# Twelve blocks' convolution on GpSimd in fp32, and stores one block late by SyncE

## The chip, the cores and the metric

The kernel runs on one core of a Trainium2 chip. Its time is the device time of one execution in microseconds (us). The kernel before takes 466.52 us, the median of 13 runs (466.1 to 467.46).

## What is computed

A causal convolution with a window of seven tokens, its weights a softmax for each of eight heads of 24 channels, and behind it a feed-forward layer whose hidden value is the greatest of three products:

```python
w = softmax(weight)                       # [8, 7]
out = einsum('hk,bskhg->bshg', w, x_unf)  # x: [8, 4160, 192], zeros ahead of each sequence
x = out.reshape(33280, 192)
h = maximum(maximum(x @ w1, x @ w2), x @ w3)   # 192 -> 768
return h @ w_out                          # 768 -> 192
```

Inputs and output are fp32.

## The kernel before

**Blocks.** The 33280 tokens are cut into 65 blocks of 512: eight from each of the eight sequences, and one more made of the last 64 tokens of every sequence (it stands at place 58). The loop at L545 takes blocks 2 to 64, one a pass; blocks 0 and 1 are done ahead of it. The order of all instructions on each engine is the order of the program text, written by hand.

**The feed-forward layer.** The maximum is computed as relu(y(w1-w3)), against y(w2-w3), and y w3 is added back through m = w3 w_out. `l1` (L390) does one sixth of the first layer of a block: TensorE multiplies the two halves of `wd` with y (L399, PSUM tiles lp and lq, two products beside each other in the two halves of the rows), ScalarE takes the relu of one (L403, to r), VectorE the maximum of r and the other (L404, to h). `st2` (L408) does one sixth of the second layer of the block before (L451, PSUM tile po); ScalarE copies one half (L460), VectorE adds the other (L461) into the output tile o. A pass t is thus `l1(t, 0..5)` interleaved with `st2(t-1, 0..5)`.

**The convolution.** Blocks 0 to 3 are convolved in another way (`conv_dense`) while the weights arrive. From block 4 on, the path of a block is:

- `load_x` (L113): SyncE loads x in eight rows of 70 tokens (64 and the six before them), six blocks ahead, into six buffers.
- `cast_x` (L147): GpSimd casts it to fp16 in two instructions (L158), five blocks ahead; where a row starts a sequence it sets six rows to zero (L155).
- `conv` (L291): TensorE multiplies it with a band matrix, 16 matmuls of 192 columns (L301), for two blocks at once (block 4 alone), three passes ahead of the first of the two. So every second pass has a convolution in it. The result lies in PSUM tiles G.
- `evac` (L342): ScalarE and VectorE cast G to fp16 tiles ys (L347).
- `turn` (L351): SyncE has the DMA engines transpose ys into yd (L358), channels on the partitions, three blocks ahead.
- `double` (L362): two copies by DMA (L366) bring each half of the partitions the tokens that the other half holds, two blocks ahead. `y_all` and `y_tok` then address the four runs of 128 tokens for L399 and L451.

**Stores.** `store(t-1)` at the end of a pass (L594) is issued by GpSimd (L480), behind that pass's casts; only the last two blocks go by SyncE and ScalarE. The output tiles o are three buffers, taken by `begin`.

**Queues.** SyncE issues, in this order within a pass, the load of t+6, the two doublings of t+2 and the transpose of t+3. Each engine waits in order: what stands behind a waiting instruction waits with it. The DMAs that SyncE issues take eight completion semaphores in turn, so a transfer is issued only when the eighth before it is complete.

Of the kernel before, what the change touches and what calls it, by code (L numbers as in the profile page):

```python
# [9 lines left out]
FP32 = mybir.dt.float32  # L10
FP16 = mybir.dt.float16
# [3 lines left out]
P = 128  # L15
KW = 7
PAD = KW - 1
NHEAD = 8
GRP = 24
# [3 lines left out]
HALF = P // 2  # L23
# [4 lines left out]
def kernel(  # L28
# [12 lines left out]
    nc = tc.nc  # L41
    ctx.enter_context(tc.manual_schedule())

    B, SEQ, D = x.shape
# [6 lines left out]
    blocks = []  # L51
    nfull = SEQ // NBLK
# [14 lines left out]
    if segs:  # L67
        blocks.append(segs)
    NB = len(blocks)
    ENDS = NB - 7  # L70
    blocks.insert(ENDS, blocks.pop())
    blkN = [sum(sg[2] for sg in blk) for blk in blocks]

    def conv_chunks(blk):
# [21 lines left out]
    xap = ctx.enter_context(tc.tile_pool(name="xap", bufs=1))  # L96
    xbp = ctx.enter_context(tc.tile_pool(name="xbp", bufs=1))
    xfp = ctx.enter_context(tc.tile_pool(name="xfp", bufs=6))
    x16p = ctx.enter_context(tc.tile_pool(name="x16p", bufs=3))
    ysp = ctx.enter_context(tc.tile_pool(name="ysp", bufs=3))  # L100
    ydp = ctx.enter_context(tc.tile_pool(name="ydp", bufs=6))
# [9 lines left out]
    xin = {}  # L111

    def load_x(t, eng=nc.sync):  # L113
        if not 0 <= t < NB:
            return
        pool, tag = (xfp, "xf") if t > 1 else ((xap, "xa"), (xbp, "xb"))[t]
        xf = pool.tile([P, NR, D], FP32, tag=tag, name=f"xf_{t}")
        if t < NDENSE:
            todo = [(0, c[3], c[1] * SEQ + c[2]) for c in chunks_of[t]]
        else:  # L120
            todo = [(PAD, HALF, b * SEQ) if s == 0 else (0, HALF + PAD, b * SEQ + s - PAD)
                    for b, s in rows_of(t)]
        parts = []
        i, n = 0, len(todo)
        row = [c[2] for c in todo]
        while i < n:
            k = i
            while k + 1 < n and todo[k + 1][:2] == todo[i][:2] and row[k + 1] - row[k] == row[i + 1] - row[i]:
                k += 1
            step = row[i + 1] - row[i] if k > i else 0  # L130
            p0, rlen = todo[i][:2]
            src = bass.AP(tensor=x.tensor, offset=row[i] * D,
                          ap=[[D, rlen], [step * D, k - i + 1], [1, D]])
            eng.dma_start(out=xf[p0:p0 + rlen, i:k + 1, :], in_=src)  # L134
            if parts and parts[-1][0] == rlen:
                parts[-1] = (rlen, parts[-1][1], k + 1)
            else:
                parts.append((rlen, i, k + 1))
            i = k + 1
        xin[t] = [xf, todo[0][0], parts]  # L140

    def place(t):
        return (t, 0, 1) if t == NDENSE else (t - (t - NDENSE - 1) % 2, (t - NDENSE - 1) % 2, 2)

    x16s, slots = {}, {}

    def cast_x(t):  # L147
        if not 0 <= t < NB:
            return
        xf, p0, _ = xin.pop(t)  # L150
        t0, u, nu = place(t)
        if u == 0:
            x16s[t0] = x16p.tile([P, NHEAD, 2, nu, NR // 2, GRP], FP16, tag="x16", name=f"x16_{t0}")
        if p0:
            nc.gpsimd.memset(xf[0:p0, 0, :], 0.0)  # L155
        K = HALF + PAD
        for c in range(2):
            nc.gpsimd.tensor_copy(out=x16s[t0][0:K, :, c, u, :, :].rearrange("p h r c -> p r h c"),  # L158
                                  in_=xf[0:K, c:NR:2, :].rearrange("p r (h c) -> p r h c", c=GRP))

    NC, NSLOT, CYC = D // HALF, D // 32, 96
    NCH = NC * NBLK // P
# [69 lines left out]
    cast_dense(0, (nc.vector.tensor_copy, nc.gpsimd.tensor_copy))  # L234
    for v in range(2):
        nc.gpsimd.memset(xz[1][v][:], 0.0)
    bps = psq.tile([32, WIN, NHEAD], FP32, tag="q", name="band_cols")
    for c in range(WIN):
        nc.tensor.matmul(bps[:, c, :], lhsT=line[:, WIN - 1 - c:WIN + 31 - c],
# [111 lines left out]
    def turn(t):  # L351


        if t >= NB:
            return
        t0, u, nu = place(t)
        yd = dense[t] = ydp.tile([P, 2, NCH // 2, P], FP16, tag="yd", name=f"yd_{t}")
        nc.sync.dma_start_transpose(out=yd[:, 0, :, :],  # L358
                                    in_=slots[t0][:, u, :, :].rearrange("p r d -> p (r d)"))
# [6 lines left out]
                nc.sync.dma_start(out=yd[HALF * i:HALF * (i + 1), 1, :, :],  # L366
                                  in_=yd[HALF * (1 - i):HALF * (2 - i), 0, :, :])

    def spot(i, f):

        return f // 2 + (0 if f % 2 == i else NCH // 2)

    def y_all(t, i, c):
        row = slice(HALF * i, HALF * (i + 1))
        if t < NDENSE:
            return dense[t][row, c, :]
        a = dense[t][row, 0, 0, :]
        s0, s1 = spot(i, c), spot(i, c + NC)
        assert all(spot(i, NC * r + c) == (s1 if r % 2 else s0) + NC * (r // 2) for r in range(4))
        return bass.AP(tensor=a.tensor, offset=a.offset + P * s0,  # L380
                       ap=[list(a.ap[0]), [P * NC, 2], [P * (s1 - s0), 2], [1, P]])

    def y_tok(t, i, c, s):
        row = slice(HALF * i, HALF * (i + 1))
        if t < NDENSE:
            return dense[t][row, c, P * s:P * (s + 1)]
        k = spot(i, NC * s + c)
        return dense[t][row, k // (NCH // 2), k % (NCH // 2), :]

    def l1(t, j, pools=((psp, "p"), (psq, "q"))):  # L390

# [93 lines left out]
    def begin(t):  # L485
        hs[t] = hp.tile([P, NJ, NBLK], FP16, tag="h", name=f"h_{t}")
        outs[t] = outp.tile([P, 4, D], FP32, tag="o", name=f"o_{t}")
# [52 lines left out]

    convs_at = {2: 4, 3: 5}
    doubles_at = {2: (), 3: (4,), 4: (5, 6)}
    for t in range(2, NB):  # L545
        if t > 4:
            load_x(t + 6)
        for u in doubles_at.get(t, (t + 2,)):
            double(u)
        if t == 4:  # L550
            load_x(t + 6)
        if t > 3:
            cast_x(t + 5)
        begin(t)
        l1(t, 0)
        if t == 2:
            conv_dense(3, (nc.scalar.copy, nc.vector.tensor_copy, nc.scalar.copy))
            cross_dma(3)
            load_x(7)
        u = convs_at.get(t, t + 3 if t % 2 == 0 else NB)  # L560
        if t > 2 and u < NB:
            st2(t - 1, 0, NJ, True)
        conv(u, PQ if t == 2 else WPWQ)
        if t == 2:
            evac(u, 0)
            evac(u, 1, nc.vector.tensor_copy)
        else:
            for i in (0, 1):
                evac(u, i)
            for i in (3, 2):  # L570
                evac(u, i, nc.vector.tensor_copy)
        if t == 2:
            turn(4)
            load_x(8)
            cast_x(5)
            cast_x(6)
        elif t == 3:
            turn(5)
            turn(6)
            load_x(9)  # L580
            cast_x(7)
            cast_x(8)
        else:
            turn(t + 3)
        st2(t - 1, 0, NJ)
        for j in range(1, NJ):
            l1(t, j)
            st2(t - 1, j, NJ)
            if t == NB - 1 and j == 3:
                store(t - 1, 0, 2, (nc.sync,))  # L590
        if t == NB - 1:
            store(t - 1, 2, 4, (nc.sync,))
        else:
            store(t - 1, 0, 4, (nc.gpsimd,))  # L594
    for u in range(NJ):
        st2(NB - 1, u, NJ)
# [28 lines left out]
```

## Time and profile before

| what | value |
|---|---|
| median of 13 runs | 466.52 us |
| time of the profiled execution | 467.46 us |
| its span, first to last instruction | 465.7 us |
| TensorE busy, of it the convolution of blocks from 4 on (L301) | 459.3, 26.1 us |
| VectorE, ScalarE, GpSimd busy | 359.7, 318.6, 163.6 us |
| GpSimd: casts of x (L158), store issues (L480) | 97.7 us x122, 48.2 us x64 |
| GpSimd waiting ahead of a store for L461 | 214.4 us |
| SyncE waiting ahead of a transpose for the evacuation (L347) | 114.3 us |
| one transpose issue, one load issue, one doubling issue on SyncE | 1.29, 0.52, 0.50 us (median, 150 to 260 us) |
| DMA: SyncE's queue, GpSimd's queue, share of 16 engines | 57.9%, 15.0% |
| moved | 81.14 MB, 174 GB/s |
| TensorE's granted clock | 1.00 throughout |

A line of the profile names line, engine and operation, then output and inputs by the program's names, with partitions x elements; "x61" is a count, the number after the bar the busy time, then the mean of one in ns, then the engine's idle time ahead of it and what ended that. In the timeline a line is start, duration, engine, line and operation, in us from the span's start. PE is TensorE (PEld its weight loads), DVE VectorE, ACT ScalarE, POOL GpSimd, SPq the issues of SyncE.

### The profile page before, as it was taken

Reading aid. Unit: us, or ns where it says so; the run is one execution under the profiler, and the core shown is the slowest. Engines: PE = TensorE matmul, PEld = TensorE weight load, DVE = VectorE, ACT = ScalarE, POOL = GpSimd, SP = SyncE. Lnnn points to the kernel's source line nnn. Section 1 sums busy time; section 2 is a strip of 40 time slices with the busy share of each in tenths; the row PEclk is TensorE's granted clock in tenths of the full one; section 3 lists DMA queues with packets and bytes.
Section 4 is the critical chain, followed back from the end, with each engine's and each line's share of the span. In section 5 each row is a group of like instructions: output and inputs, shape, how many; then the busy total and the mean of one; then the engine's idle time right before and its main releaser. Section 6 shows DMA issues by size and latency. Waiting matters only on the chain.

```text
span 465.7 us, 17191 instructions
## 1 busy us (share of the span) xinstructions
PE 459.3 (99%) x7065; PEld 372.0 (80%) x7065; DVE 359.7 (77%) x607; ACT 318.6 (68%) x609; POOL 163.6 (35%) x227
## 2 busy tenths in 40 slices
PE   8899999999999999999999999999999999999996
PEld 4487878788788888878788887878888787887886
DVE  7778777877878777777777877778778787787775
ACT  5766767667666676676766767676676766766664
POOL 5664343244234324423424432432442343243010
PEclk9999999999999999999999999999999999999999
DMA  8949987778687777888766868778686976774512
GB/s 199 236 115 196 216 211 188 174 196 176 166 212 183 151 186 176 184 180 198 184 148 194 175 175 197 174 176 188 171 183 165 208 171 167 183 169 107 119 69 103
DMA packets 107114, 81.14 MB, mean 174 GB/s; under 512 B 53110, under 2 KB 101980, under 8 KB 107036
## 3 DMA queue, kind: packets, MB, share of 16 engines
q1 hardware_dynamic: 99804, 55.17, 57.9%
q0 software_dynamic: 7072, 24.78, 15.0%
q8 instruction: 55, 0.90, 0.9%
q14 instruction: 23, 0.19, 0.1%
q10 hardware_dynamic: 160, 0.10, 0.1%
HBM read 30.28 MB, written 25.56 MB: 120 GB/s over the span
## 4 chain that ended last, share of the span: by engine, by line
PE 94%; DMA 3%; SPq 2%; issue 0%; POOL 0%; DVE 0%; ACT 0%
PE lq L399 38%; PE po L451 36%; PE lp L399 15%; PE G L301 6%; DMA wos<-in_moe_w_out_dram 3%; SPq L190 1%; PE D L319 0%; SPq L134 0%; POOL wo L525 0%; PE pm L280 0%; PE pm L284 0%; DVE o L461 0%; ACT a L460 0%
## 5 line engine op out<-in xcount | busy, mean ns | idle before, releaser
L404 DVE TENSOR_TENSOR h<-r,lq 128x512 f16<-128x512 f16 x386 | 264.7, 686 | 98.4 <-ACT r L403 97.9
L403 ACT ACTIVATE r<-lp 128x512 f16<-128x512 f32 x386 | 230.5, 597 | 134.5 <-PE lp L399 122.9
L399 PE MATMUL lp<-yd,wd 64*128 64x512 f16 x1158 | 312.2, 376 | 0.7 <-DVE wd L256 0.5
L399 PE MATMUL lq<-yd,wd 64*128 64x512 f16 x1158 | 312.1, 376 | 0.0
L451 PE MATMUL po<-wo,h 64*128 64x192 f16 x3120 | 262.6, 243 | 0.0
L451 PEld LDWEIGHTS <-h 64*128 64x128 f16 x3120 | 208.4, 94 | 20.5
L399 PEld LDWEIGHTS <-wd 64*128 64x128 f16 x2340 | 161.9, 94 | 37.2 <-issue 1.4
L480 POOL DMA_DIRECT2D out_dram<-o x64 | 48.2, 753 | 280.6 <-DVE o L461 214.4
L451 PE MATMUL po<-m,yd 64*128 64x192 f16 x780 | 109.5, 243 | 0.0
L158 POOL CAST x<-xf 70x768 f16<-70x768 f32 x122 | 97.7, 835 | 2.3 <-PE po L451 1.8
L461 DVE TENSOR_TENSOR o<-a,po 128x384 f32<-128x384 f32 (+1 forms) x132 | 71.3, 541 | 0.6 <-ACT a L460 0.6
L451 PEld LDWEIGHTS <-yd 64*128 64x128 f16 x780 | 61.7, 94 | 12.0
L460 ACT COPY a<-po 128x384 f32<-128x384 f32 (+1 forms) x132 | 62.2, 472 | 2.1 <-PE po L451 2.1
L347 DVE CAST ys<-G 128x384 f16<-128x384 f32 x61 | 31.0, 549 | 0.0
L301 PEld LDWEIGHTS <-band 70*64 70x64 f16 x496 | 19.5, 109 | 11.5 <-PE lp L399 11.4
L347 ACT CAST ys<-G 128x384 f16<-128x384 f32 x61 | 26.2, 482 | 0.0
L301 PE MATMUL G<-x,band 70*64 70x192 f16 (+1 forms) x496 | 26.1, 248 | 0.0
L215 PE MATMUL idle<-idle 128*128 128x512 f16 x15 | 6.5, 578 | 1.2 <-DVE idle L210 1.2
L177 POOL CAST xz<-xf 112x80 f16<-112x80 f32 (+2 forms) x18 | 5.2, 332 | 4.0 <-DMA xf<-in_x_dram 3.2
L319 PEld LDWEIGHTS <-xz 112*32 112x32 f16 x240 | 4.6, 107 | 2.1 <-POOL xz L177 0.8
L319 PE MATMUL D<-band,xz 112*32 112x103 f16 (+1 forms) x240 | 5.3, 229 | 0.0
L335 DVE COPY yd<-yd 64x512 f16<-64x512 f16 x9 | 4.2, 468 | 0.5 <-ACT yd L325 0.2
(45 smaller groups left out, 52.0 us busy)
## 6 DMA issues: line engine op xcount, KB each, us to landing
xf<-in_x_dram SPq DMA_DIRECT2D x57, 420.0 KB
out_dram<-o POOLq DMA_DIRECT2D x62, 384.0 KB, 3.7
yd<-yd SPq DMA_DIRECT2D x122, 96.0 KB
xf<-in_x_dram SPq DMA_DIRECT2D x7, 367.5 KB
ws<-in_moe_w_dram SPq DMA_DIRECT2D x6, 192.0 KB
yd<-ys SPq DMA_TRANSPOSE x61
w3s<-in_moe_w_dram SPq DMA_DIRECT2D x3, 192.0 KB
wos<-in_moe_w_out_dram SPq DMA_DIRECT2D x1, 576.0 KB
```

The costliest lines, as they stand in the source:

```text
L158: nc.gpsimd.tensor_copy(out=x16s[t0][0:K, :, c, u, :, :].rearrange("p h r c -> p r h c"), in_=xf[0:K, c:NR:2, :].rearrange("p r (h c) -> p ...
L215: nc.tensor.matmul(ps[:], lhsT=idle[:, 0:P], rhs=idle[:], start=True, stop=True)
L301: nc.tensor.matmul(G[h // per][HALF * c:HALF * (c + 1), h % per, :], lhsT=band[0:HALF + PAD, h, PAD:HALF + PAD], rhs=x16s[t0][0:HALF + PAD ...
L319: nc.tensor.matmul(ps[32 * g:32 * g + 32, lo:hi], lhsT=xz[t][v][0:rlen, q, 32 * s:32 * s + 32], rhs=band[0:rlen, h, cc:cc + hi - lo], star ...
L347: copy(out=slots[t][:, :, :, GRP * per * i:GRP * per * (i + 1)].rearrange("p u r (h c) -> p h (u r) c", c=GRP), in_=G[i][:].rearrange("p h ...
L399: nc.tensor.matmul(ps[i][:, 0:N], lhsT=wd[row, c, P * j:P * (j + 1)], rhs=y_all(t, i, c), start=(c == 0), stop=(c == NC - 1))
L403: nc.scalar.activation(out=r[:, 0:N], in_=ps[0][:, 0:N], func=AF.Relu)
L404: nc.vector.tensor_max(out=hs[t][:, j, 0:N], in0=r[:, 0:N], in1=ps[1][:, 0:N])
L451: nc.tensor.matmul(ps[b0, i][:, s % 2, :], lhsT=a, rhs=b, start=first, stop=last)
L460: nc.scalar.copy(out=a[:, ss, :], in_=ps[s0, 0][:, ss, :])
L461: nc.vector.tensor_add(out=outs[t][:, s0:s + 1, :], in0=a[:, ss, :], in1=ps[s0, 1][:, ss, :])
L480: qs[0].dma_start(out=bass.AP(tensor=out.tensor, offset=r * D, ap=[[D, n], [step * D, s1 - s0], [1, D]]), in_=ob[p0:p0 + n, s0:s1, :])
```

## The change

Twelve blocks leave the path above: those at places 11, 16, 21, ... 61 and 64. The eight blocks of the last sequence and four of the one before it are put there in their order, so that each block finds the end of the one before it in its sequence. The others keep their path in 24 pairs and block 4 alone; the convolution of a pair still comes three passes ahead of its first.

A block q of the twelve is loaded as four rows of 128 tokens without overlap (`load_q`), into the buffers of blocks 0 and 1. GpSimd casts it (`cast_q`), SyncE transposes it before the convolution (`turn_q`), so that tokens lie along the free axis, and copies the six tokens ahead of each run into a strip in front (`lead_q`; a small copy on GpSimd does the strips of the odd runs). Then GpSimd computes a tap at a time (`tap_q`): three multiplications of 128x256 by a number for each partition, fp16 to fp32, and from the second tap on an addition of 128x768 in fp32; the last addition writes yd in fp16. Doubling, `l1` and `st2` are as for the others.

The load is issued six passes ahead of the first tap, the casts three, the transpose two, the strips one. The taps are spread over five passes as 2, 1, 2, 1, 1 and end three passes before the block is used. The first of the twelve (11) is loaded in pass 2 behind the loads of blocks 7 and 8, cast in pass 3, transposed in pass 4, and its taps lie in passes 5 to 8 as 2, 2, 2, 1. The last (64) has its taps in passes 58 to 61. The weights by channel (`spread_w`) go through DRAM in passes 3 and 4.

The stores of all blocks but block 0 are now issued by SyncE, a pass later: `store(t-2)` behind the transpose of pass t.

```diff
...
     NB = len(blocks)
+    EVERY = 5
+    qpos = [q for q in range(11, NB - 3, EVERY)] + [NB - 1]
+    qset = set(qpos)
     ENDS = NB - 7
-    blocks.insert(ENDS, blocks.pop())
+    ends = blocks.pop()
+    lanes = blocks[-nfull:] + blocks[-2 * nfull:-nfull]
+    lanes, rest = lanes[:len(qpos)], [blk for blk in blocks if blk not in lanes[:len(qpos)]]
+    rest.insert(ENDS - sum(q < ENDS for q in qpos), ends)
+    blocks = [(lanes if t in qset else rest).pop(0) for t in range(NB)]
     blkN = [sum(sg[2] for sg in blk) for blk in blocks]
...
     xfp = ctx.enter_context(tc.tile_pool(name="xfp", bufs=6))
+    xqp = ctx.enter_context(tc.tile_pool(name="xqp", bufs=2))
+    xtp = ctx.enter_context(tc.tile_pool(name="xtp", bufs=3))
+    accp = ctx.enter_context(tc.tile_pool(name="accp", bufs=2))
     x16p = ctx.enter_context(tc.tile_pool(name="x16p", bufs=3))
...
     def load_x(t, eng=nc.sync):
-        if not 0 <= t < NB:
+        if not 0 <= t < NB or t in qset:
             return
...
         xin[t] = [xf, todo[0][0], parts]
+    pairs, left = {}, [t for t in range(NDENSE + 1, NB) if t not in qset]
+    assert len(left) % 2 == 0
+    for a in left[::2]:
+        b = left[left.index(a) + 1]
+        assert b == a + 1
+        pairs[a], pairs[b] = (a, 0, 2), (a, 1, 2)
+    pairs[NDENSE] = (NDENSE, 0, 1)
     def place(t):
-        return (t, 0, 1) if t == NDENSE else (t - (t - NDENSE - 1) % 2, (t - NDENSE - 1) % 2, 2)
+        return pairs[t]
     x16s, slots = {}, {}
     def cast_x(t):
-        if not 0 <= t < NB:
+        if not 0 <= t < NB or t in qset:
             return
...
                                   in_=xf[0:K, c:NR:2, :].rearrange("p r (h c) -> p r h c", c=GRP))
+    LEAD = 16
+    xqs, xts = {}, {}
+    def load_q(q):
+        pool, tag = ((xap, "xa"), (xbp, "xb"))[qpos.index(q) % 2]
+        xf = pool.tile([P, NR, D], FP32, tag=tag, name=f"xl_{q}")
+        (b, S, N, _), = blocks[q]
+        nc.sync.dma_start(out=xf[:, 0:N // P, :],
+                          in_=bass.AP(tensor=x.tensor, offset=(b * SEQ + S) * D,
+                                      ap=[[D, P], [P * D, N // P], [1, D]]))
+        xin[q] = xf
+    def cast_q(q):
+        xf = xin.pop(q)
+        xqs[q] = xqp.tile([P, 3, 2, 2, HALF], FP16, tag="xq", name=f"xq_{q}")
+        for i in range(2):
+            nc.gpsimd.tensor_copy(out=xqs[q][:, :, :, i, :].rearrange("p c r m -> p r c m"),
+                                  in_=xf[:, 2 * i:2 * i + 2, :].rearrange("p r (c m) -> p r c m", m=HALF))
+    def turn_q(q):
+        xt = xts[q] = xtp.tile([P, 6, LEAD + P], FP16, tag="xt", name=f"xt_{q}")
+        nc.sync.dma_start_transpose(out=xt[:, :, LEAD:LEAD + P],
+                                    in_=xqs.pop(q)[:].rearrange("p c r i m -> p (c r i m)"))
+    def lead_q(q):
+        xt, n = xts[q], qpos.index(q)
+        prev = qpos[n - 1] if n and blocks[q][0][1] > 0 else None
+        T = LEAD + P
+        if prev is None:
+            nc.gpsimd.memset(xt[0:HALF, 0:6:2, LEAD - PAD:LEAD], 0.0)
+        else:
+            nc.sync.dma_start(out=xt[0:HALF, 0:6:2, LEAD - PAD:LEAD],
+                              in_=xts[prev][HALF:P, 1:6:2, T - PAD:T])
+        nc.sync.dma_start(out=xt[HALF:P, 0:6:2, LEAD - PAD:LEAD], in_=xt[0:HALF, 1:6:2, T - PAD:T])
+    accs = {}
+    def tap_q(q, k):
+        xt = xts[q]
+        if k == 0:
+            T = LEAD + P
+            nc.gpsimd.tensor_copy(out=xt[:, 1:6:2, LEAD - PAD:LEAD], in_=xt[:, 0:6:2, T - PAD:T])
+        part = accp.tile([P, 6, P], FP32, tag="t" if k else "a", name=f"tap{k}_{q}")
+        for c in range(3):
+            nc.gpsimd.tensor_scalar(out=part[:, 2 * c:2 * c + 2, :],
+                                    in0=xt[:, 2 * c:2 * c + 2, LEAD - PAD + k:LEAD - PAD + k + P],
+                                    scalar1=wcol[:, c, k:k + 1], scalar2=0.0,
+                                    op0=mybir.AluOpType.mult, op1=mybir.AluOpType.add)
+        if k == 0:
+            accs[q] = part
+            return
+        if k < KW - 1:
+            nc.gpsimd.tensor_add(out=accs[q][:], in0=accs[q][:], in1=part[:])
+            return
+        yd = dense[q] = ydp.tile([P, 2, NCH // 2, P], FP16, tag="yd", name=f"yd_{q}")
+        nc.gpsimd.tensor_add(out=yd[:, 0, :, :], in0=accs.pop(q)[:], in1=part[:])
     NC, NSLOT, CYC = D // HALF, D // 32, 96
...
         nc.gpsimd.memset(xz[1][v][:], 0.0)
+    wcol16 = const.tile([P, 3, KW], FP16)
+    wcol = const.tile([P, 3, KW], FP32)
+    wide = dram.tile([D, KW], FP16, name="wide")
+    def spread_w(part):
+        if part == 0:
+            nc.sync.dma_start(out=wide[:].rearrange("(h c) k -> h c k", c=GRP),
+                              in_=line[:, 31:31 + KW].unsqueeze(1).to_broadcast([NHEAD, GRP, KW]))
+        elif part == 1:
+            for i in range(2):
+                nc.sync.dma_start(out=wcol16[HALF * i:HALF * (i + 1), :, :],
+                                  in_=wide[:].rearrange("(c p) k -> p c k", p=HALF))
+        else:
+            nc.gpsimd.tensor_copy(out=wcol[:], in_=wcol16[:])
     bps = psq.tile([32, WIN, NHEAD], FP32, tag="q", name="band_cols")
...
     def turn(t):
-        if t >= NB:
+        if t >= NB or t in qset:
             return
...
                                   in_=yd[HALF * (1 - i):HALF * (2 - i), 0, :, :])
-    def spot(i, f):
-
-        return f // 2 + (0 if f % 2 == i else NCH // 2)
+    def spot(t, i, c, r):
+        if t in qset:
+            own, k = r // 2, 2 * c + r % 2
+        else:
+            own, k = (NC * r + c) % 2, (NC * r + c) // 2
+        return k + (0 if own == i else NCH // 2)
     def y_all(t, i, c):
...
+        k = spot(t, i, c, s)
+        return dense[t][row, k // 6, k % 6, :]
     def l1(t, j, pools=((psp, "p"), (psq, "q"))):
...
-    convs_at = {2: 4, 3: 5}
+    convs_at = {2: 4, 3: 5, 4: 7}
+    convs_at.update({t - 3: t for t in pairs if t > 8 and pairs[t][1] == 0})
     doubles_at = {2: (), 3: (4,), 4: (5, 6)}
+    plan = {}
+    for n, q in enumerate(qpos):
+        w = min(4 + EVERY * n, NB - 7)
+        load, cast, turned, lead = (1, 3, 4, 4) if n == 0 else (w - 6, w - 3, w - 2, w - 1)
+        when = {0: (5, 5, 6, 6, 7, 7, 8), len(qpos) - 1: [w + k // 2 for k in range(KW)]}.get(
+            n, [w + k * EVERY // KW for k in range(KW)])
+        for what, at in (("load", load), ("cast", cast), ("turn", turned), ("lead", lead)):
+            plan.setdefault(at, {})[what] = q
+        for k in range(KW):
+            plan.setdefault(when[k], {}).setdefault("taps", []).append((q, k))
     for t in range(2, NB):
+        todo = plan.get(t, {})
         if t > 4:
...
             load_x(t + 6)
+        if t > 3 and "turn" in todo:
+            turn_q(todo["turn"])
+        if t > 4 and "lead" in todo:
+            lead_q(todo["lead"])
         if t > 3:
             cast_x(t + 5)
+        if "load" in todo:
+            load_q(todo["load"])
         begin(t)
...
             load_x(7)
-        u = convs_at.get(t, t + 3 if t % 2 == 0 else NB)
+        u = convs_at.get(t, NB)
         if t > 2 and u < NB:
...
             load_x(8)
+            load_q(plan[1]["load"])
             cast_x(5)
...
             turn(t + 3)
+        if t == 3:
+            spread_w(0)
+        if t == 4:
+            spread_w(1)
+            lead_q(todo["lead"])
+        if 2 < t:
+            store(t - 2, 0, 4, (nc.sync,))
+        if "cast" in todo:
+            cast_q(todo["cast"])
+        for q, k in todo.get("taps", ()):
+            if q == qpos[0] and k == 0:
+                spread_w(2)
+            tap_q(q, k)
         st2(t - 1, 0, NJ)
...
             store(t - 1, 2, 4, (nc.sync,))
-        else:
-            store(t - 1, 0, 4, (nc.gpsimd,))
     for u in range(NJ):
```

More of the change, by code (lines that the diff above doesn't have):

```diff
@@ L377, in y_all @@
         a = dense[t][row, 0, 0, :]
-        s0, s1 = spot(i, c), spot(i, c + NC)
-        assert all(spot(i, NC * r + c) == (s1 if r % 2 else s0) + NC * (r // 2) for r in range(4))
+        s0, s1, s2, s3 = (spot(t, i, c, r) for r in range(4))
+        assert s3 - s2 == s1 - s0
         return bass.AP(tensor=a.tensor, offset=a.offset + P * s0,
-                       ap=[list(a.ap[0]), [P * NC, 2], [P * (s1 - s0), 2], [1, P]])
+                       ap=[list(a.ap[0]), [P * (s2 - s0), 2], [P * (s1 - s0), 2], [1, P]])
     def y_tok(t, i, c, s):
@@ L386, in y_tok @@
             return dense[t][row, c, P * s:P * (s + 1)]
-        k = spot(i, NC * s + c)
-        return dense[t][row, k // (NCH // 2), k % (NCH // 2), :]
+        k = spot(t, i, c, s)
+        return dense[t][row, k // 6, k % 6, :]
     def l1(t, j, pools=((psp, "p"), (psq, "q"))):
```

## Prediction

> **What bounds the kernel now.** I read the page first, its busy times and its chain of work.
>
> ```profile
> PE 459.3 (99%) x7065; PEld 372.0 (80%) x7065; DVE 359.7 (77%) x607; ACT 318.6 (68%) x609; POOL 163.6 (35%) x227
> ...
> PE 94%; DMA 3%; SPq 2%; issue 0%; POOL 0%; DVE 0%; ACT 0%
> PE lq L399 38%; PE po L451 36%; PE lp L399 15%; PE G L301 6%; DMA wos<-in_moe_w_out_dram 3%; SPq L190 1%; PE D L319 0%; SPq L134 0%; POOL wo L525 0%; PE pm L280 0%; PE pm L284 0%; DVE o L461 0%; ACT a L460 0%
> ```
>
> TensorE carries the chain; 6% of it is the convolution (G, L301). A busy TensorE need not be at its peak, so I then looked at GpSimd's timeline in the middle of the run, because its store closes each pass of the block loop and so works as a clock.
>
> ```profile
> 195.47 0.75 POOL L480 DMA_DIRECT2D out_dram<-o  x1 [4.01 <-PE G L301]
> 196.22 1.60 POOL L158 CAST x<-xf 70x768 f16<-70x768 f32 x2
> 202.78 0.75 POOL L480 DMA_DIRECT2D out_dram<-o  x1 [4.97 <-DVE o L461]
> ...
> 209.15 0.75 POOL L480 DMA_DIRECT2D out_dram<-o  x1 [3.71 <-DVE o L461]
> 209.90 1.60 POOL L158 CAST x<-xf 70x768 f16<-70x768 f32 x2
> 216.51 0.75 POOL L480 DMA_DIRECT2D out_dram<-o  x1 [5.01 <-DVE o L461]
> ```
>
> The passes take 7.31, 6.37, 7.36 us: passes with and without a convolution alternate, and the difference is 1.0 us. GpSimd works 2.4 us of a pass and waits 4 to 5. The same stretches as windows (busy time, then granted clock, DMA share, GB/s):
>
> ```profile
> 202.78:209.15 6.37, 6.37 (x103) 4.89 (x100) 4.88 (x9) 4.84 (x10) 2.60 (x5) 1.00 0.87 220
> 209.15:216.51 7.36, 7.36 (x114) 6.49 (x112) 5.81 (x11) 4.65 (x9) 2.35 (x4) 1.00 0.82 182
> ```
>
> The clock is full (1.00) and TensorE never idle. Over 60 to 420 us the DMA share is 0.77. So a pass is worth what TensorE streams in it, as long as GpSimd, SyncE and the DMAs stay within it.
>
> **The change, part by part.**
>
> *TensorE.* Of the blocks from 4 on, 61 are convolved now: one alone and 30 pairs. Twelve leave, 48 remain in 24 pairs: six pair convolutions fewer, that is 96 matmuls and 96 weight loads at L301. The chain shows one such convolution as 0.85 us (x16); with the switch of weights before and after it the passes differ by 1.0. 6 x 1.0 = 6.0 us less, all of it on the path. The matmuls of L399 read a GpSimd block in another order of four runs of 128; dense blocks (one run of 512) and the others both show 376 ns, so I take nothing for it. ScalarE and VectorE lose 24 casts (482 and 549 ns), which is off the path.
>
> *GpSimd, steady state.* It loses 63 of its 64 store issues of 0.75 us (47.4; block 0's stays) and the casts of twelve blocks (12 x 1.67 = 20). It gains, per block, two casts of half the size, one tiny copy, 21 scalar multiplications of 128x256, six additions of 128x768 in fp32. Rows near:
>
> ```profile
> L256 POOL TENSOR_TENSOR wd<-ws,w3s 128x768 f16<-128x768 f32 x1 | 1.8, 1813 | 0.9 <-DMA ws<-in_moe_w_dram 0.9
> ...
> L256 DVE TENSOR_TENSOR wd<-ws,w3s 128x768 f16<-128x768 f32 x1 | 1.0, 953 | 0.0
> ...
> L208 POOL CAST ident<-ident 128x128 f16<-128x128 f32 x1 | 0.3, 291 | 0.1
> ```
>
> An addition: 1.81 us, the same size and fp32 inputs, so 6 x 1.81 = 10.9. A multiplication has no row. Below: one-input casts, 128 elements in 0.29 and 768 in 0.835, interpolate to 0.41. Above: the two-input row scaled to 256 elements (0.60) with 0.1 fixed, 0.71. It has one tensor input, so I take 0.42: 21 x 0.42 = 8.8 (up to 14.9). Casts 2 x 0.5, copy 0.1. A block: 20.8 us (up to 27). The schedule gives it five passes. Those hold also four ordinary casts, 4 x 1.67 = 6.7, and an occasional memset 0.25: 27.8 us. Five passes with two convolutions last 3 x 6.36 + 2 x 7.36 = 33.8. It fits, with 6 us to spare. Pass by pass too: the fullest has two taps (3 x 0.42 + 1.81 = 3.07 each) and a cast, or two taps and the next block's casts: 7.1 to 7.8 us against 7.36, made good in the next pass with one tap. An ordinary cast is issued at the head of a pass and needed by the convolution one pass later at the earliest, which hides lags of up to about 4 us.
>
> Here the Trainium skill speaks against the change: "GPSIMD Engine Reference", section 4.1, says to put elementwise work on VectorE, GpSimd being about twice as slow with two inputs. The rows agree on the ratio (1813 against 953 ns). But by duration alone VectorE would get some 2 us more per pass of a 4.9 to 5.8 us load in 6.4 to 7.4, while GpSimd gets 250 us that replace 67, beside 302 us of idleness. The rule prices the instruction; the sum prices the path, where it is 0. A second one, "SBUF — State Buffer", "Who interferes with whom", on the port pair that VectorE and GpSimd share: a VectorE instruction with two SBUF inputs and a GpSimd instruction that reads SBUF block each other fully. If L404 (386 of 686 ns) fell under it, up to 0.69 us would be added to each addition, 4 us per block, still inside the 6 us. But its second input is PSUM, and GpSimd's 1813 ns addition at 17.21 us ran beside two L404 at 17.18 and 18.05, which took 0.69 each: I take 0.
>
> *SyncE and the DMAs.* Per five passes: five stores, about 0.55 us of issue each (as the other transfers), two small halo copies for the window's edge 1.1; transposes and doublings stay as many. SyncE issues about 3.0 us per pass now, 3.8 then. A store of block t-2 waits for L461, done 1.1 us into the pass; behind it are the next load and doubling, which have a pass. Its tile is written again two passes later: about 7 us of slack. Doubling a GpSimd block waits for its last tap, two passes ahead of its use; behind that wait stands the next transpose, also two passes ahead. DMA time: a store took 0.96 us of 16 engines through GpSimd (share of the windows 443 to 445), and half of one 0.59 through SyncE (458 to 460), so +0.2 each; halo copies between 0 and 1.2 per five passes (384 pieces at no more than an x row's price); x 512 rows in place of 560, -0.15. 26.4 of 34.3 us become 28 to 28.7 of 33.8: share 0.83 to 0.85. Hidden, if tighter.
>
> *The start.* Here the cover is thin.
>
> ```profile
> 45.00:52.00 7.00, 7.00 (x108) 6.12 (x104) 5.44 (x11) 4.41 (x9) 2.10 (x3) 1.00 1.07 227
> 52.00:59.00 7.00, 7.00 (x112) 5.80 (x109) 5.52 (x10) 5.08 (x10) 2.88 (x4) 1.00 0.97 198
> 59.00:66.00 7.00, 7.00 (x109) 5.63 (x107) 5.49 (x10) 4.59 (x9) 2.04 (x4) 1.00 1.04 234
> ```
>
> The DMAs are full to about 66 us. Two loads of 393 KB (blocks 11 and 16) now stand in the queue ahead of the doublings of blocks 4 and 5: 1.9 us each at 208 GB/s, less the 1 us of a store that comes later. In the trace those doublings' packets end at 41.7 and about 46.6; TensorE wants them at 42.88 and 50.25. They become about 42.6 and 49.6, plus the notice: between 0 and 1.5 us of wait, I take 0.4.
> Then GpSimd: block 11's first tap needs its halo. SyncE issues that only when its transpose has landed, behind block 6's doubling (about 47), the load of 10, two transposes and the weight copies: issued near 55, landed near 57 (54 to 58.5). Behind the first tap, in order, stand taps 0 to 5, block 16's casts and the ordinary casts of 12 and 13: 1.3 + 5 x 3.07 + 1.0 + 2 x 1.67 = 21.0. So block 13 is ready near 78 (75 to 83). The convolution of 12 and 13 stands at 57.49 + 7.36 + 2 x 6.36 = 77.6, plus the 0.4. It waits 0 to 5 us; with a little for the waits between dependent GpSimd instructions I take 0.9. Later convolutions find the lag caught up.
>
> **Sum.** -6.0 + 0.4 + 0.9 = -4.7. On the profiled execution (span 465.7, time 467.46, 1.8 around the span) that makes 462.8; it lay 0.94 above the median of 466.52, so for the median 461.8.
>
> **The rivals.**
> *No loss at the start:* DMAs at the speed of the quiet stretches, halo at 54: 466.5 - 6.0 = 460.5. For it: transposes there run faster than I queue them. Chance 0.17.
> *More lag at the start, steady state as said:* tap near 3.6 us or halo near 59, block 13 late by 3 to 5 us: 463 to 465.6. Chance 0.15.
> *Slower: GpSimd becomes the bound.* With u us per multiplication, five passes cost it 21u + 19 us. At u = 0.71 that is the 33.8 us of five passes after, at 0.73 the 34.3 of five before: from there each further 0.1 costs 2.1 us times eleven blocks. At u = 0.9: 37.9, +3.6 x 11 = 40, near 506. At 0.73 the start alone takes 6 us back. For it: no row for a multiplication by a per-partition number with fp16 in and fp32 out, at odd offsets. Against: the cast of 768 elements in 0.835. Chance 0.12.
> *Likeliest,* 460.7 to 463: 0.51. Around no change 0.05.
> A measurement of this kernel tells about 0.2% (0.9 us) from nothing. Faster 0.83, the same 0.05, slower 0.12. The range 460.1 to 465.7 reaches from no loss to the long lag and leaves GpSimd as bound out.
>
> **What would show it.** TensorE's L301 in 24 groups of about 0.85 us in the chain, plus block 4's; passes of 6.36 and 7.36 in the ratio 3 to 2; GpSimd near 346 us busy (75%), multiplications near 0.42 and additions near 1.8 us, and hardly a wait of L301 for GpSimd except at the first pairs after 70 us; L404 still 0.69; DMA share near 0.85. Wrong would be: multiplications over 0.7 us, waits of L301 for L158 again and again, or waits of L399 for doublings after 66 us.

## The result, and the profile after

The kernel after takes 463.29 us, the median of 11 runs (462.48 to 464.92), beside 466.73 for the kernel before in the same comparison: a ratio of 0.9926 [0.991, 0.9941], 3.4 us less. Its profiled execution took 464.55 us (span 462.8), 2.9 less than that of before (467.46, span 465.7). The profiled execution of after lies 1.26 above its median; that of before lay 0.94 above the 466.52 of its 13 runs.

The page after, its busy times and its chain of work by engine and line:

```profile
PE 454.3 (98%) x6969; PEld 368.0 (80%) x6969; DVE 354.4 (77%) x595; ACT 314.6 (68%) x597; POOL 353.6 (76%) x501
...
PE 88%; POOL 5%; DMA 4%; SPq 1%; issue 1%; DVE 0%; ACT 0%; POOLq 0%; DVEq 0%
```

TensorE lost 96 matmuls and 5.0 us of busy time. GpSimd has 353.6 us of work, and it and the DMAs now hold 9% of the chain. Where that is, TensorE's waits show (total, times, longest):

```profile
PE lp L499 <- DMA yd<-yd: 1.5, 2, 1.0
PE G L397 <- POOL x L176: 1.3, 2, 0.8
```

These are four waits in 463 us; the few others that the profile shows end before 25 us, as they do before. The timeline of TensorE, cut to these four and to convolutions, puts them between 43 and 81 us (the bracket is the idle time and what ended it):

```profile
43.20 0.39 PE L499 MATMUL lp<-yd,wd 64*128 64x512 f16 x1 [0.54 <-DMA yd<-yd]
...
44.17 0.85 PE L397 MATMUL G<-x,band 70*64 70x192 f16 x16
...
51.85 0.39 PE L499 MATMUL lp<-yd,wd 64*128 64x512 f16 x1 [0.95 <-DMA yd<-yd]
...
59.28 0.85 PE L397 MATMUL G<-x,band 70*64 70x192 f16 x16
...
80.14 0.24 PE L397 MATMUL G<-x,band 70*64 70x192 f16 x1 [0.76 <-POOL x L176]
80.91 0.82 PE L397 MATMUL G<-x,band 70*64 70x192 f16 x15 [0.53 <-POOL x L176]
...
114.64 0.85 PE L397 MATMUL G<-x,band 70*64 70x192 f16 x16
...
148.40 0.85 PE L397 MATMUL G<-x,band 70*64 70x192 f16 x16
```

From 114.64 to 148.40 are five passes: 33.76 us, the 33.8 of the prediction. The convolutions serve as milestones, because before has the same ones up to blocks 9 and 10. The convolution of 5 and 6 starts at 35.82 (before: 36.40, so after is 0.58 ahead). That of 9 and 10 starts at 59.28 (before: 57.49). Between them after has lost **2.37 us** to the doublings of blocks 4 and 5. From there to the convolution of 14 and 15 (94.50) it takes 35.22, where undisturbed passes make 33.76: another **1.46 us**, to GpSimd. The ledger: -0.58 + 2.37 + 1.46 - 6.0 = -2.75, beside spans that differ by 2.9. (From the convolution of 9 and 10 to the end, before takes 408.2 us and after 403.5 with the 1.46 in it: the six convolutions that are gone measure 6.15.) The two doubling waits show 1.5 us of idle time but cost 2.37. Some 0.2 us of each is overlap: before, L399 at 42.88 starts while the matmuls from 42.47 are still in flight to 43.07, and a wait takes that away. The rest was not traced.

SyncE's timeline shows when it issues the doublings of blocks 5 and 6 (x4), first before:

```profile
42.99 2.38 SPq L366 DMA_DIRECT2D yd<-yd  x4
```

and after, with three issues ahead of them that were not there before:

```profile
39.91 0.59 SPq L188 DMA_DIRECT2D xl<-in_x_dram  x1
...
44.89 0.84 SPq L324 DMA_DIRECT2D wide<-line  x1
45.78 0.47 SPq L580 DMA_DIRECT2D out_dram<-o  x1
46.35 3.65 SPq L462 DMA_DIRECT2D yd<-yd  x4
```

They go out 3.4 us later: a load, a copy of the weights and a store take 1.9 us of issue ahead of them, and SyncE is 1.1 us late already at the doubling of block 4 (38.73, before 37.62). From the issue to the end of TensorE's wait at block 5 are 5.5 us more. How much of the delay is SyncE's order and how much slower copying was not separated.

The chain of work after, over the first 82 us, names what led to the GpSimd wait:

```profile
44.05 0.18 SPq L454
...
50.73 5.69 DMA xt<-xq
56.48 2.50 DMA xt<-xt
59.16 2.77 POOL tap L229 x6
62.01 1.80 POOL tap L237
63.81 0.90 POOL xq L198 x2
...
79.33 1.54 POOL x L176 x2
80.91 0.82 PE G L397 x15
```

Block 11's transpose takes 5.69 us in the crowded DMAs, its strip lands at 58.98, and from there GpSimd works without a pause until block 13's cast is done. That is the queue the prediction described, later by 2 to 3 us.

This chain leaves TensorE at 44.0 us and goes over SyncE, block 11's transpose and GpSimd to 80.91: the wait at block 5 is not on it. So 2.37 and 1.46 are no two separate prices. Of the 2.37, 1.44 are lost at block 5 (44.17 to 59.28, where before takes 13.67 us). Without them TensorE would have come to the convolution of 12 and 13 at 77.9 in place of 79.36, and waited that much longer for the same cast (an estimate from these lines). Whichever is later, GpSimd's queue or the doublings, sets the end of the start. The groups of the costliest instructions after:

```profile
L504 DVE TENSOR_TENSOR h<-r,lq 128x512 f16<-128x512 f16 x386 | 264.7, 686 | 99.4 <-ACT r L503 98.5
...
L229 POOL TENSOR_SCALAR tap<-xt,wcol 128x256 f32<-128x256 f16 x252 | 116.8, 482 | 2.9 <-DMA xt<-xt 2.1
L237 POOL TENSOR_TENSOR tap<-tap,tap 128x768 f32<-128x768 f32 x60 | 108.7, 1811 | 5.0
```

A multiplication is 482 ns by itself (three in a row take 1.39 us, 0.46 each), an addition 1811. VectorE's maximum keeps its 686 ns beside them.

### The profile page after: what moved, and what is told of

Same layout as the page of the kernel before. It is cut to its first block, busy times and chain, and to the rows that moved or that the text cites. A ratio compares the mean times of both kernels' runs of the same rounds, so it can differ in the third digit from the quotient of the medians.

```text
span 462.8 us, 17259 instructions
## 1 busy us (share of the span) xinstructions
PE 454.3 (98%) x6969; PEld 368.0 (80%) x6969; DVE 354.4 (77%) x595; ACT 314.6 (68%) x597; POOL 353.6 (76%) x501
## 4 chain that ended last, share of the span: by engine, by line
PE 88%; POOL 5%; DMA 4%; SPq 1%; issue 1%; DVE 0%; ACT 0%; POOLq 0%; DVEq 0%
PE lq L499 34%; PE po L551 32%; PE lp L499 14%; PE G L397 4%; POOL tap L237 2%; POOL tap L229 2%; DMA yd<-ys 1%; PE idle L294 1%; DMA xt<-xq 1%; PE D L415 1%; DMA yd<-yd 1%; SPq L462 1%; POOL x L176 1%; DMA xt<-xt 1%; PE lw L499 0%
## 5 line engine op out<-in xcount | busy, mean ns | idle before, releaser
L504 DVE TENSOR_TENSOR h<-r,lq 128x512 f16<-128x512 f16 x386 | 264.7, 686 | 99.4 <-ACT r L503 98.5
L176 POOL CAST x<-xf 70x768 f16<-70x768 f32 x98 | 78.1, 825 | 63.1 <-DMA xf<-in_x_dram 55.8
L229 POOL TENSOR_SCALAR tap<-xt,wcol 128x256 f32<-128x256 f16 x252 | 116.8, 482 | 2.9 <-DMA xt<-xt 2.1
L237 POOL TENSOR_TENSOR tap<-tap,tap 128x768 f32<-128x768 f32 x60 | 108.7, 1811 | 5.0
L443 DVE CAST ys<-G 128x384 f16<-128x384 f32 x49 | 24.9, 549 | 1.2 <-PE G L397 1.2
L397 PEld LDWEIGHTS <-band 70*64 70x64 f16 x400 | 15.8, 109 | 10.6 <-PE lp L499 9.1
L240 POOL TENSOR_TENSOR yd<-tap,tap 128x768 f16<-128x768 f32 x12 | 21.8, 1813 | 1.0
L397 PE MATMUL G<-x,band 70*64 70x192 f16 (+1 forms) x400 | 21.2, 247 | 1.3 <-POOL x L176 1.3
L443 ACT CAST ys<-G 128x384 f16<-128x384 f32 x49 | 21.0, 482 | 1.4 <-PE G L397 1.4
L198 POOL CAST xq<-xl 128x384 f16<-128x384 f32 x24 | 11.5, 506 | 0.0
```

What stands on the lines that cost most here:

```text
L229: nc.gpsimd.tensor_scalar(out=part[:, 2 * c:2 * c + 2, :], in0=xt[:, 2 * c:2 * c + 2, LEAD - PAD + k:LEAD - PAD + k + P], scalar1=wcol[:, ...
L237: nc.gpsimd.tensor_add(out=accs[q][:], in0=accs[q][:], in1=part[:])
L240: nc.gpsimd.tensor_add(out=yd[:, 0, :, :], in0=accs.pop(q)[:], in1=part[:])
L397: nc.tensor.matmul(G[h // per][HALF * c:HALF * (c + 1), h % per, :], lhsT=band[0:HALF + PAD, h, PAD:HALF + PAD], rhs=x16s[t0][0:HALF + PAD ...
L443: copy(out=slots[t][:, :, :, GRP * per * i:GRP * per * (i + 1)].rearrange("p u r (h c) -> p h (u r) c", c=GRP), in_=G[i][:].rearrange("p h ...
L504: nc.vector.tensor_max(out=hs[t][:, j, 0:N], in0=r[:, 0:N], in1=ps[1][:, 0:N])
```

## The experiments

Medians are beside the kernel before on the same chip. "First stretch" is what the profiled execution lost between the convolutions of 5/6 and 9/10 against before's 21.09 us; "second" what it lost from 9/10 to 14/15 against 33.76.

**Stores alone.** The kernel before, with only the stores moved to SyncE.

```diff
+        if 2 < t:
+            store(t - 2, 0, 4, (nc.sync,))
...
-        else:
-            store(t - 1, 0, 4, (nc.gpsimd,))
```

> The kernel before, with its stores a block late by SyncE and nothing else. Start theory (the stores are hidden; what the change gave back is lost in its first 80 us): as before, 466.7 us within 0.4, DMA share in mid-run up by 0.02 to 0.03. Steady theory (stores and fuller DMA queues of SyncE slow every pass a little): 1 to 2 us slower, 467.7 to 468.7.

466.08 us against 466.6, 0.9989 [0.9975, 1.0003]; no wait for doublings, first stretch 0.0. The moved stores alone cost and bring nothing that this can tell.

**Loads behind.** The loads of 11 and 16 a step later in SyncE's order.

```diff
-        load, cast, turned, lead = (1, 3, 4, 4) if n == 0 else (w - 6, w - 3, w - 2, w - 1)
+        load, cast, turned, lead = (1, 3, 4, 4) if n == 0 else (w - 6 + 2 * (n == 1), w - 3, w - 2, w - 1)
...
-            load_q(plan[1]["load"])
...
+            load_q(plan[1]["load"])
```

The second pair of lines moves the load of 11 from behind that of 8 to behind that of 9.

> The changed kernel, with the loads of blocks 11 and 16 moved out of the way of the first doublings: 11 behind the load of 9 in pass 3, 16 in pass 5. Start theory: TensorE's two waits for doublings (about 2.2 us) go, and GpSimd's first tap begins about 2 us earlier, so that its wait for block 13 stays near 1.5: 461.1 us. If the halo comes no earlier the wait for block 13 takes the gain back and it stays at 463.3. Steady theory: 463.3.

465.04 us, 0.9967 [0.9954, 0.998]: a miss by 4 us. The wait at block 4 is gone; the one at block 5 is longer. TensorE's timeline:

```profile
51.99 0.39 PE L499 MATMUL lp<-yd,wd 64*128 64x512 f16 x1 [2.10 <-DMA yd<-yd]
```

The windows of the same kernel (busy time of PE, PEld, DVE, ACT, POOL, then granted clock, DMA share, GB/s):

```profile
50.00:52.00 2.00, 0.01 (x1) 0.01 (x1) 1.14 (x2) 0.33 (x1) 1.07 (x3) 1.00 0.81 211
52.00:54.00 2.00, 2.00 (x19) 1.51 (x21) 0.53 (x1) 0.60 (x1) 1.47 (x3) 0.69 1.35 200
54.00:56.00 2.00, 2.00 (x18) 1.49 (x16) 0.69 (x2) 0.60 (x1) 0.81 (x2) 0.50 1.01 154
56.00:58.00 2.00, 2.00 (x33) 1.44 (x28) 0.89 (x3) 1.32 (x3) 1.15 (x5) 0.96 0.33 51
```

The doubling of 5 lands when it did (51.99 beside 51.85). What were two short waits is one long one, and behind it the clock falls to 0.50: 19 and 18 matmuls in 2 us in place of 33. The first stretch loses 4.16, the second nothing: GpSimd has block 13's cast ready at 80.67, as late as in after (80.86), but TensorE itself comes only at 81.00. My theory that the place of the loads was the fault falls here.

**Taps later.** Block 11's taps a little later, so that the ordinary casts come first.

```diff
-        when = {0: (5, 5, 6, 6, 7, 7, 8), len(qpos) - 1: [w + k // 2 for k in range(KW)]}.get(
+        when = {0: (5, 6, 7, 7, 8, 8, 8), len(qpos) - 1: [w + k // 2 for k in range(KW)]}.get(
```

> The changed kernel, with the seven taps of block 11 in passes 5 to 8 as 1, 1, 2, 3 in place of 2, 2, 2, 1, so that four and not six stand ahead of the cast of block 13. Start theory: that cast ends near 74.5 us, ahead of TensorE's 79.4, and the wait of the convolution of 12 and 13 (1.5 us) goes; later ones find their casts: 461.8 us, doublings' waits as they were. Steady theory: 463.3.

463.9 us, 0.9947 [0.9934, 0.996]: a miss by 2 us, and not to be told from after. In its profile the wait of 12 and 13 is gone and one of 0.4 us has come at 14 and 15; the first stretch still loses 2.32.

**Both.** The two edits together.

> Both edits, loads behind and taps later. Start theory: no wait of TensorE is left after 40 us but what it had before, and the six convolutions show whole: 466.7 - 6.0 = 460.7, or 463.3 - 3.7 = 459.6 by the waits. Steady theory: no less than 462.5.

464.92 us, 0.9974 [0.9963, 0.9985]: missed. First stretch 4.48 (one wait of 2.3 us, clock 0.57 and 0.58 in the 4 us behind it), second 0.

**Loads in the gap.** Both loads at the head of pass 2.

```diff
...
+            load_q(qpos[0])
+            load_q(qpos[1])
...
-            load_q(plan[1]["load"])
```

> The changed kernel with one thing moved: the loads of blocks 11 and 16 are issued at the beginning of pass 2, right behind the load of 6 and ahead of the copies for block 3, where SyncE waits and the DMAs are little used (25 to 31 us), and no longer in passes 2 and 3. Queue theory (TensorE waits for the doublings of blocks 4 and 5 because those two loads and a store stand ahead of them in SyncE's queue): both waits go, 2.2 us, and the first tap begins about 2 us earlier with its wait behind it: 461.1, or 460.7 if the wait for block 13 goes too. Rival (the DMAs are simply short of time up to 66 us, wherever the loads stand, or the halo and weight copies slow them): no better than 463.

465.87 us, 0.997 [0.9954, 0.9986]: missed. Most of its 22 runs lie near 463.4 or near 466.2, one at 461.45; the profiled one took 466.07. The doublings' waits are gone (first stretch 0.0), but not because these come sooner: SyncE issues those of 5 and 6 at 46.66, and TensorE is itself late, with the convolution of 5 and 6 at 39.66 in place of 35.82. Its timeline shows the wait that made it late:

```profile
31.22 0.28 PE L397 MATMUL G<-x,band 70*64 70x96 f16 x4 [2.46 <-issue]
```

"Issue" names no releaser. The DMA queue that carries instructions brought pieces of 16 KB at 26.1 and 29.8 us before and after, and at 28.9 and 34.5 here, so I infer that TensorE waited for its own code behind the loads; no run tests that. The clock then shows 0.50 from 32 to 34 us, and the second stretch loses 1.51 to GpSimd as in after.

**Two taps.** Taps 1 to 5 left out.

```diff
+            if 0 < k < KW - 1:
+                continue
```

> The changed kernel without taps 1 to 5 of the twelve blocks: GpSimd multiplies by the first and the last weight only and adds once, the rest of the convolution of these blocks is left out. DMAs and TensorE have the work of the changed kernel. If GpSimd costs time only by the wait of the convolution of 12 and 13: 1.5 us less, 461.8. If its work slows others in every pass (a shared port, memory): 460 or less.

462.66 us, 0.9922 [0.9902, 0.9941]. First stretch 1.63, second 0. With 191 us of GpSimd's work gone (162.9 busy in place of 353.6) the median moves by 0.6 us, where 1.5 were expected and the runs of both spread over 2.4 us or more. So that work is hidden but for the start.

**One multiplication more** per tap.

```diff
-        for c in range(3):
+        for c in (0, 1, 2, 0):
```

> The changed kernel, one of the three multiplications of every tap issued twice (same values again): 7 x 0.464 = 3.25 us more of GpSimd per block. Five passes then take GpSimd 28.7 + 3.3 = 32.0 us of 33.8: still hidden in mid-run. Ahead of the cast of block 13 stand six of them, 2.8 us: 466.1. If the wait at the start is not on the path: 463.3. If GpSimd is the bound already: 463.3 + 11 x 3.25 = 499.

469.5 us, 1.0056 [1.0027, 1.0086]: slower than before. TensorE's timeline, then the windows behind it:

```profile
81.84 0.32 PE L397 MATMUL G<-x,band 70*64 70x192 f16 x1 [3.18 <-POOL x L176]
```

```profile
82.00:84.00 2.00, 1.55 (x18) 1.11 (x18) 0.00 (x0) 0.86 (x2) 2.00 (x5) 0.50 0.97 280
84.00:86.00 2.00, 2.00 (x17) 1.58 (x18) 1.02 (x2) 0.00 (x0) 1.92 (x2) 0.50 0.17 36
86.00:88.00 2.00, 2.00 (x19) 1.61 (x17) 0.69 (x1) 0.60 (x1) 1.95 (x4) 0.53 0.23 49
88.00:90.00 2.00, 2.00 (x34) 1.81 (x32) 1.25 (x3) 1.56 (x3) 1.95 (x5) 1.00 0.76 150
```

The waits for GpSimd grow from 1.3 to 3.6 us, as expected, and 6 us at half clock follow, which nothing had foreseen: the second stretch loses 6.4. After it no convolution waits for GpSimd. Seven more multiplications per block (3.2 us) still fit into the middle of the run; at the start the six of them that stand ahead of block 13's cast (2.8 us) turn the gain into a loss.

**All multiplications twice.**

```diff
+        for c in (0, 1, 2, 0, 1, 2):
```

> The changed kernel, all multiplications issued twice (same values again): 9.7 us more per block, so five passes take GpSimd 38.4 us against TensorE's 33.8. By the price of the rival in the prediction GpSimd is then the bound in every group of five passes: 4.6 us each, ten to eleven times, and some 8 us at the start: 510 to 522 us. If slack elsewhere takes part of it: under 500.

520.87 us, 1.1171 [1.1146, 1.1197]. TensorE's waits:

```profile
PE G L397 <- POOL x L176: 31.8, 29, 8.4
```

GpSimd is the bound (90% busy), and the waits recur through the run. This is the slower rival's mechanism, at about its price: 42 x 0.464 + 19 = 38.5 us for five passes is 4.7 over 33.76, times eleven 52; measured 57.6 over after, with a mean clock of 0.957. The clock falls here behind shorter waits than elsewhere, where two of them stand close together (TensorE's timeline, then a window behind it):

```profile
125.93 0.24 PE L397 MATMUL G<-x,band 70*64 70x192 f16 x1 [1.69 <-POOL x L176]
126.70 1.44 PE L397 MATMUL G<-x,band 70*64 70x192 f16 x15 [0.53 <-POOL x L176]
```

```profile
128.00:130.00 2.00, 2.00 (x18) 1.51 (x18) 1.02 (x2) 0.08 (x1) 1.92 (x5) 0.50 0.04 12
```

**First of the twelve later.** Load of 11 behind the doublings of pass 4, its cast, transpose, strips and taps later, 16 later too.

```diff
...
-        load, cast, turned, lead = (1, 3, 4, 4) if n == 0 else (w - 6, w - 3, w - 2, w - 1)
+        load, cast, turned, lead = (0, 4, 0, 0) if n == 0 else (w - 6 + 2 * (n == 1), w - 3, w - 2, w - 1)
-        when = {0: (5, 5, 6, 6, 7, 7, 8), len(qpos) - 1: [w + k // 2 for k in range(KW)]}.get(
+        when = {0: (5, 6, 7, 7, 8, 8, 8), 1: (9, 10, 10, 11, 11, 12, 13), len(qpos) - 1: [w + k // 2 for k in range(KW)]}.get(
...
```

> The changed kernel with the first block's GpSimd path moved behind what the start needs: the load of 11 behind the doublings of 5 and 6 (pass 4), of 16 in pass 5; cast, transpose and halo of 11 half a pass to a pass later; taps of 11 as 1, 1, 2, 3 and of 16 as 1, 2, 2, 1, 1. Ahead of the doublings stand then only what stood there in the run with the stores alone, which showed no wait; the instruction fetches of the first 30 us are left alone. Start theory (work ahead of the doublings, code fetch and GpSimd's order are all that the start loses): no wait of TensorE over 0.5 us after 30 us and a clock of 1.00: 460.7, 460 to 461.5. If the start loses time wherever these loads go: 463 or more.

465.09 us, 0.9972 [0.995, 0.9994]: missed. The doublings cost the first stretch 1.07, but block 11's load, issued at 52.3, landed near 58 and its first tap started at 67.67, so the next three convolutions waited for GpSimd (2.0 us in four waits). This execution (467.76, one of the slower) also lost 2.3 us near 16 us to a weight. Every place tried for the load moved a wait and removed none for good.

**Stores back on GpSimd.** After, with the stores as before.

```diff
-        if 2 < t:
-            store(t - 2, 0, 4, (nc.sync,))
...
+        else:
+            store(t - 1, 0, 4, (nc.gpsimd,))
```

> The changed kernel with the stores as before: by GpSimd at the end of the pass, none by SyncE but the last. Five passes then cost GpSimd 28.7 + 5 x 0.75 = 32.5 us of 33.8, and it waits for the end of every pass before it goes on, so a lag in the two fullest passes (up to 1.4 us) is never worked off ahead of time; the store of block 1 no longer stands ahead of the doublings. If GpSimd has to run ahead for the convolutions to find their casts: waits of L397 in most groups of passes, 470 or more. If the slack of one pass between cast and convolution is enough: 462 to 464, and the stores' move was not needed.

468.03 us, 1.0029 [1.0007, 1.0051]. The profiled execution (466.42, one of the quicker) loses 3.63 and 1.98 in the two stretches and nothing in the middle, where GpSimd is 87% busy: 1.8 more than after, which is its whole difference in time to after's (466.42 - 464.55). The medians differ by 4.7; what the slower executions add, this profile doesn't show, nor why the doublings' waits are longer (1.13 and 1.69 us). So the moved stores, worth nothing alone, are needed once GpSimd convolves.

**Ten blocks.** Places 11 and 16 go back to TensorE.

```diff
-    qpos = [q for q in range(11, NB - 3, EVERY)] + [NB - 1]
+    qpos = [q for q in range(21, NB - 3, EVERY)] + [NB - 1]
...
```

> The changed kernel with ten blocks on GpSimd in place of twelve: places 11 and 16 go back to TensorE, the first is 21, on the schedule of the later ones; stores by SyncE as changed. Nothing is added to the DMAs or to GpSimd in the first 70 us. If the start is where the change loses (theory): five pair convolutions fewer, 5.0 us, and no wait for doublings or for GpSimd: 466.1 (stores alone) - 5.0 = 461.1, 460.6 to 462. If the loss is spread over all passes: 463.3 + 1.0 = 464.3.

464.51 us (462.44 to 468.1), 0.9955 [0.9931, 0.9978]. The profiled execution, the fastest of the twelve, fits: no wait for a doubling or for GpSimd, first stretch 0.39, span 460.7 for five pair convolutions fewer. The median doesn't; what spreads the others I did not find. It is not shown to be better than after.

**Loads alone.** The stores-alone kernel with two unused loads of 393 KB where after has those of 11 and 16.

```diff
+    def load_q(t, n):
+        pool, tag = ((xap, "xa"), (xbp, "xb"))[n]
+        xf = pool.tile([P, NR, D], FP32, tag=tag, name=f"xl_{t}")
...
```

> The kernel before with its stores a block late by SyncE, and two more loads of 393 KB at the places where the changed kernel loads blocks 11 and 16; what they load is not used, all else is as in the run with the stores alone (466.1). If 786 KB more in the first 50 us are what delays the doublings: TensorE waits for those of blocks 4 and 5, 1.5 to 2.5 us together: 467.6 to 468.6. If the waits came from the weight copies, the transpose of 11 or GpSimd: 466.1.

467.89 us, 1.0022 [1.0002, 1.0041], 1.8 above stores alone, as expected. The profiled execution is the slowest of the twelve: 470.59, 4.16 above that of stores alone, and 4.16 is what its first stretch loses. TensorE's timeline:

```profile
51.94 0.60 PE L407 MATMUL lp<-yd,wd 64*128 64x512 f16 x1 [2.36 <-DMA yd<-yd]
```

The matmul is 0.60 long in place of 0.38 because the clock has fallen (0.50 from 52 to 54 us). Without any GpSimd convolution, the two loads alone hold up block 5 until 51.94, where after has 51.85. So the two loads by themselves are enough for the wait at block 5, in this slow execution; block 4's wait, the other part of after's loss, does not appear (its convolution of 7 and 8 comes 7.42 us behind that of 5 and 6, as before). In this kernel SyncE issues the doublings of 5 and 6 at 45.19, without a copy of the weights ahead of them; in stores alone at 42.56.

## Why the prediction was right, and which terms were off

It said -4.7 to a median of 461.8; measured were -3.4 and 463.29. The direction and the mechanism held. The median is 0.3 us outside the likeliest branch and inside that of more lag at the start, and one of that branch's two signs came: a strip (the halo) near 59 us, measured 58.98. The other, a tap near 3.6 us, did not (3.27).

- *TensorE, -6.0:* held. Five passes last 33.76, and no wait interrupts them after 82 us; from the convolution of 9 and 10 on, 6.15 us less were measured, GpSimd's 1.46 apart.
- *GpSimd in the middle at 0:* held, with its sizes near. A multiplication took 0.46 to 0.48 (0.42 taken, 0.71 as upper bound), an addition 1.81; 353.6 us busy beside 346. The shared-port rule that was weighed did not bite: L504 took 678 to 691 ns, beside additions or not. One multiplication more per tap still fits in the middle; doubling them makes GpSimd the bound.
- *Stores on SyncE and the DMAs at 0:* held in the middle (DMA share 0.83 over 60 to 420 us; stores alone 466.08). The stores' move is however part of the cover: back on GpSimd they cost 1.8 in the profile and 4.7 in the median.
- *Doublings, 0.4:* mis-sized. The first stretch lost 2.37 and, set against before's own times, 1.79 (59.28 - 57.49; the other 0.58 is a start that was earlier). Block 5's doubling was expected near 49.6, "between 0 and 1.5 us of wait"; it came in time for 51.85. The step that was mis-sized is the sum of bytes over 208 GB/s for one transfer in a full queue. It has no term for SyncE, which issued these doublings 3.4 us later than before, and it left out that TensorE then waits twice and that each wait costs more than its idle time. Loads alone show that the two loads suffice for the wait at block 5; that they make the one at block 4 is not shown.
- *GpSimd's queue at the start, 0.9:* 1.46. The first tap started at 59.16 (57 taken, up to 58.5), because the transpose took 5.69 us, and five further taps took 0.2 us more each. Block 13 was ready at 80.86, within the 75 to 83 given. That only 1.46 came of it is luck in part: against the 78.0 at which the prediction had TensorE there, it would have been a wait of 2.9 us, but the doublings had made TensorE late too (79.36). Taps later and two taps remove this wait or nearly so.

Together 1.3 foreseen and 3.8 lost in the profile, of which 0.58 may only give back an earlier start (not tested). The median shows half a microsecond less loss than that; the waits differ from execution to execution (0.59 and 0.76 for the doublings in one profile of taps later, a single 0.65 in two taps).

That better places for the two loads would win back these 2 to 3 us was my theory after the result, and it fell in four kernels. One reason is in the traces: a TensorE that is late at block 5 (loads behind, both) hides GpSimd's queue, and one that is late already at 31 us (loads in the gap) hides the doublings. What stays besides: from 31 to 66 us the DMAs are busy 0.82 to 1.07 of the time in after, and 786 KB more are paid for by a doubling, by block 11's own transpose, or probably by the instructions. Which of the twelve blocks' gains could be had without it stays open: ten blocks reached 462.44 once, and no more in the median.

## What to carry to other kernels

Work that was moved to an idle engine was free in the steady state here, where its time for a period was less than the period, and the sum from rows of like size came within 3% (346 us foreseen, 353.6 busy). The start is where it was paid: look there for the first consumer of every new transfer, of every place in the new engine's queue and of every place in the issuing engine's order, and cost a wait with what follows it. Where two lags meet at one instruction, the later one counts, and shortening one alone brings at most the difference. Shifting two loads within a full DMA queue helped in none of four places; taking them out of that stretch removed the waits in one profile (ten blocks), though the median gained nothing.

## What the runs showed of the hardware

- TensorE's granted clock fell behind long waits, and the length of a wait did not decide it alone. Behind single waits of 0.54 to 1.69 us (after, one multiplication more, stores back on GpSimd) it stayed at 1.00. Behind every single one of 2.10 us or more it fell, to 0.50 to 0.58 in the lowest window of 2 us, for some 3 to 6 us: 2.10 (loads behind), 2.30 (first of the twelve later), 2.34 (both), 2.36 (loads alone), 2.46 (loads in the gap) and 3.18 us (one multiplication more). That costs about as much again as the wait. Behind two waits with one matmul between them it went either way: 0.76 and 0.53 us in after and 1.29 and 0.52 in stores back on GpSimd left it at 1.00; in all multiplications twice 0.88 and 0.53 brought it to 0.50, and 1.67 and 0.53 once did not. What decides there was not found. The Trainium skill, "TensorE: Matmul & The Clock Gate", section "What's actually happening", puts the fall to half rate after at least one idle window of about 3.4 us; here waits a third shorter sufficed. Two waits 9 us apart were cheaper than one: 1.13 and 1.69 us lost 3.63 us in stores back on GpSimd, a single 2.10 lost 4.16 in loads behind.
- A GpSimd multiplication of 128x256, fp16 to fp32, by a number for each partition takes 482 ns.
